# Retention and a gated MLP in one kernel: the first positions' values loaded by position in fp32 by another queue, with keys, queries and idle products rearranged to match

## The chip, the cores and the metric

The kernel runs on one core of one Trainium2 chip. A core has TensorE (PE; its weight loads are listed as PEld), VectorE (DVE), ScalarE (ACT), GpSimd (POOL) and SyncE (SP, which here only issues transfers). [...] The metric is the device time of one execution in microseconds (us), as the median of several runs.

## What is computed

```python
B, H, S, D = 8, 8, 576, 64               # q, k, v: fp32 [B, H, S, D]
scores = D ** -0.5 * q @ k.T             # for each batch and head
gamma[h] = 1 - 2 ** (-5 - h)
ret = scores * (gamma[h] ** (i - j) where i >= j, else 0)
x = (ret @ v) put together as [B * S, H * D]      # 4608 x 512
h = x @ w_in                             # w_in  512 x 2048
g = h * clip(h + 3, 0, 6) / 6
out = g @ w_out                          # w_out 2048 x 512
```

## The kernel before, in words

The 576 positions of a batch are split into the first 64 (the code calls them heads, `TL` is 64) and four chunks of 128. The first 64 positions of all eight batches make up block 0 of 512 tokens; the eight blocks after it are one batch each. A block goes through attention, then through the up-products `ph` (PE, 16 units of 128 columns of `w_in`, each four pairs of 128x512 matmuls; ACT and DVE make `u` and `g` from each), then through the down-products `pd` or `pm` with `w_out`. For the blocks after block 0, attention inside a chunk is done directly, and what lies before the chunk comes from a running state. The state left by the first 64 positions is made by `head_states` from block 0's keys and values.

Each engine takes its instructions in exactly the order in which the code issues them (a manual schedule); strings such as "k0 D4 k1 D4 ... h0" write the order out by hand, where `k` is `keys_heads`, `h` is `head_states`, `D` is a down-product step, `c` casts a loaded chunk, `t` turns it. An engine that waits holds up all that is behind it in its own list, and that holds for the issue of transfers too.

What comes ahead of the first up-product is the start of the kernel, and the change is almost wholly there:

- `load_half` (L403-416) loads the first 64 positions of head pair `i`, for two heads one after the other. A row of a transfer is four positions of one batch, 1 KB. Key pair 0 and the queries come as fp32 by SP and ACT and are cast by DVE (`cast_heads`). Keys of the pairs 1 to 3 and all values come by POOL, cast to fp16 on the way. `after` makes a transfer wait until another one has landed: most wait until key pair 0 has (`keys`).
- The partition of such a tile is batch and position group, so `turn_heads` (L428-440) uses matmuls with a permutation (`by_chunk`) to get the head dimension onto partitions, sorted into four chunks of two batches each; ACT or DVE copies the result out of PSUM.
- `by_key` (L441-449) permutes the other way with 16 small matmuls for each pair: values into `vh` (`values_heads`, by an ACT copy of 128x512), and later keys into `kn` (`keys_heads`, two ACT multiplies of 128x512, each with one of the two batches set to zero by `only`). The rows of a chunk are then in the order of position group, batch, position, and the masks (`distances`, `mask_of_heads`) are made for that order. `others` (L138-145) multiplies the keys by their decay on POOL ahead of that.
- `scores_heads` (PE `hpa`, DVE's multiply by the mask), `inner_heads` (PE `hpo`, which needs all four chunks of `vh`, and a copy into `xT`), then the first four up units in turn.
- `idle_products` are PE matmuls of an identity whose result nobody reads.
- `win_piece` and `wout_piece` issue the eight pieces of the MLP's weights by POOL. `fetch` loads the chunks of the later blocks by SP; the first one waits until the third piece of `w_out` to be issued has landed.

Of the kernel before, what the change touches and what calls it, by code (L numbers as in the profile page):

```python
# [14 lines left out]
I32 = mybir.dt.int32  # L15
# [6 lines left out]
def kernel(  # L22
# [45 lines left out]
    ii = const.tile([P, NJ + 1], I32)  # L68
    ij = const.tile([P, NJ + 6], I32)
    fj = const.tile([P, NJ + 6], FP32)  # L70
    key, odd = fj[:, NJ + 3:NJ + 4], fj[:, NJ + 5:NJ + 6]
    arg = const.tile([P, NJ + 3, 2 * H], FP32)
    dec = const.tile([P, NJ + 3, 2 * H], FP32)
# [11 lines left out]
    only = const.tile([P, 2], FP32)  # L85
# [4 lines left out]
    def indices():  # L90
        nc.vector.memset(half, 0.5)
        nc.gpsimd.iota(ii[:, 0:NJ], pattern=[[0, NJ]], base=0, channel_multiplier=1)
        nc.gpsimd.iota(ii[:, NJ:NJ + 1], pattern=[[1, 1]], base=0, channel_multiplier=1)
# [3 lines left out]
        p_ = ii[:, NJ:NJ + 1]  # L97
        nc.vector.tensor_scalar(ij[:, 0:NJ], ii[:, 0:NJ], P - B, 1, ALU.bitwise_and, ALU.logical_shift_right)
        nc.vector.tensor_copy(ij[:, NJ:NJ + 1], p_)
        for e in range(2):  # L100
            nc.vector.tensor_scalar(ij[:, NJ + 1 + e:NJ + 2 + e], p_, SUB - 1, 1, ALU.bitwise_and,
                                    ALU.logical_shift_left)
        nc.vector.tensor_scalar(ij[:, NJ + 3:NJ + 4], p_, RP - 1, 2, ALU.bitwise_and, ALU.logical_shift_left)
        nc.vector.tensor_scalar(ij[:, NJ + 4:NJ + 5], p_, 5, None, ALU.logical_shift_right)
        nc.vector.tensor_scalar(ij[:, NJ + 5:NJ + 6], p_, 4, 1, ALU.logical_shift_right, ALU.bitwise_and)
        nc.vector.tensor_copy(fj, ij)
        nc.vector.tensor_tensor(fj[:, 0:NJ], fj[:, 0:NJ], query[:, 0:TL:RP], ALU.add)
        nc.vector.tensor_scalar(fj[:, NJ:NJ + 2], fj[:, NJ:NJ + 2], 1.0, -float(P // 2), ALU.mult, ALU.add)
        nc.vector.tensor_scalar(fj[:, NJ + 2:NJ + 3], fj[:, NJ + 2:NJ + 3], 1.0, 1.0 - float(P // 2), ALU.mult, ALU.add)
        nc.vector.tensor_copy(by_chunk.rearrange("p (c e r) -> p c e r", c=NCB, e=2),  # L110
                              ident16.rearrange("p (r e c) -> p c e r", e=2, c=NCB))

    def distances():
        nc.vector.memset(scale, float(np.log(D ** -0.5)))
        nc.vector.tensor_tensor(key, key, fj[:, NJ + 4:NJ + 5], ALU.add)
        nc.vector.scalar_tensor_tensor(out=key, in0=odd, scalar=float(TL), in1=key, op0=ALU.mult, op1=ALU.add)
# [11 lines left out]
    def decays():  # L128
        for h in range(H):
            lg = float(np.log(gamma[h]))  # L130
            nc.gpsimd.tensor_scalar(arg[:, :, h], fj[:, 0:NJ + 3], lg, float(np.log(D ** -0.5)),
                                    ALU.mult, ALU.add)
            nc.gpsimd.tensor_scalar(arg[:, :, H + h], fj[:, 0:NJ + 3], -lg, 0.0, ALU.mult, ALU.add)
        nc.scalar.activation(dec, arg, ACTF.Exp)
        nc.gpsimd.tensor_copy(only[:, 1:2], odd)
        nc.gpsimd.tensor_scalar(only[:, 0:1], odd, -1.0, 1.0, ALU.mult, ALU.add)

    def others():  # L138
        for i in range(NP):
            k16 = hd[i]["k"].rearrange("p e j d -> p j e d")  # L140
            dd = dec[:, 0:NJ, H + 2 * i:H + 2 * i + 2].unsqueeze(3).to_broadcast([P, NJ, 2, D])
            nc.gpsimd.tensor_tensor(k16, k16, dd, ALU.mult)
# [54 lines left out]
    def casts(c):  # L197
        dd = dec.unsqueeze(3).to_broadcast([P, NJ + 3, 2 * H, D])
# [5 lines left out]
        if c % 2 == 0:  # L204
            q16 = work.tile([P, 2, NP, 2, D], FP16, tag="q16", bufs=2, name=f"q16_{c}")
            for e in range(2):
                nc.gpsimd.tensor_tensor(by_head(q16[:, e]), in_rows(st[c]["fq"][:, :, e, :]),  # L207
                                        in_rows(dd[:, NJ + 1 + e, 0:H, :]), ALU.mult)
            st[c]["q16"] = q16
        nc.gpsimd.tensor_tensor(v16, st[c]["fv"], dd[:, NJ, H:2 * H, :], ALU.mult)  # L210
# [75 lines left out]
    def head_states(c):  # L286
        pu = psum.tile([P, 2, NP, D], FP32, tag="pp", name=f"pu{c}")
        for e in range(2):
            for i in range(NP):
# [4 lines left out]
        nc.scalar.copy(zh[c + NCB], pu[:, 1])  # L294
        nc.vector.tensor_tensor(zh[c], pu[:, 0], decay, ALU.mult)
        nc.gpsimd.tensor_tensor(zh[c + NCB], zh[c + NCB], decay, ALU.mult)
# [98 lines left out]
    kn = [ws[n].rearrange("p j n -> p (j n)").rearrange("p (i c x) -> p i c x", i=NP, c=NCB) for n in (1, 2)]  # L395
# [32 lines left out]
    def turn_heads(i, nm, copy):  # L428
# [5 lines left out]
        x, y = (NCB, 2 * RP) if nm == "k" else (2 * NCB, RP)  # L434
        t = half_tile(work, "qT", i, FP16, "hqT", bufs=3) if nm == "q" else work.tile(
            [P, H * D], FP16, tag="kT", bufs=4, name=f"hkT{i}")
        t = t.rearrange("p (x j y) -> p x j y", x=x, j=NJ)
        copy(t, pt.rearrange("p j (x y) -> p x j y", y=y))  # L438
        hd[i][nm + "T"] = t

    def by_key(i, nm):  # L441

        pv = psum.tile([P, NCB, 2, D], FP32, tag="pp", name=f"hp{nm}{i}")
        for c in range(NCB):
            for j in range(NJ):
                o = slice(2 * RP * j, 2 * RP * j + 2 * RP)
                nc.tensor.matmul(pv[o, c], by_chunk[:, 2 * RP * c:2 * RP * c + 2 * RP], hd[i][nm][:, :, j],  # L447
                                 start=True, stop=True)
        return pv

    def values_heads(i):
        nc.scalar.copy(vh[:, :, i], by_key(i, "v"))

    def keys_heads(i):
        pk = by_key(i, "k").rearrange("p c e d -> p c (e d)")
        for e in range(2):
            nc.scalar.mul(kn[e][:, i], pk, only[:, e:e + 1])

    def scores_heads(i):
# [3 lines left out]
        for c in range(NCB):  # L463
            for h2 in range(2):
                r = slice(h2 * D, h2 * D + D)
                nc.tensor.matmul(pa[h2][:, c, :], kT[r, c].rearrange("d j x -> d (j x)"),
                                 qT[r, 2 * c:2 * c + 2].rearrange("d e j r -> d (e j r)"), start=True, stop=True)
# [186 lines left out]
    def win_piece(n, parts=1):  # L654
        a, b = pieces_in[n]
        for i in range(parts):
            cc = slice(NP // parts * i, NP // parts * (i + 1))
            nc.gpsimd.dma_start(win16[n][:, cc], win_v[:, cc, BLK * a:BLK * b])
# [62 lines left out]
    with tc.manual_schedule(engines={ENG.PE, ENG.DVE, ENG.Pool, ENG.Activation, ENG.SP}):  # L721
# [47 lines left out]
        win_piece(1)  # L769
        values_heads(3)  # L770
# [15 lines left out]
        others()  # L786
# [78 lines left out]
```

## Time and profile before

| What | Value |
|---|---|
| median of 3 runs | 301.76 us (301.63 to 302.48) |
| the profiled execution, its own time | 302.47 us |
| its span in the profile | 300.7 us |
| PE busy | 288.2 us, 96% |
| DVE, ACT, POOL busy | 213.2, 196.2, 135.5 us |
| mean granted clock of PE | 0.989 of full speed |
| first up-product | 18.51 us |
| granted clock 0.5 | 14.19 to 21.01 us |
| first `fetch` | 33.50 us |

How to read the profile: times are from the start of the span. A line of the order in time gives the start, the length, the engine, the source line, the operation, the tile written and the tiles read, partitions x elements and type, and how many; in brackets stands how long the engine was idle before and what ended that. Engines overlap, and matmuls overlap each other, so groups of PE start before the one ahead of them is listed as ended. The granted clock is the share of full speed that PE was allowed. Of a DMA queue the profile gives packets, megabytes written and the time of the packets as a share of 16 engines; an engine can have more than one packet under way, so shares go over 100%. q0 is POOL's queue, q1 SP's, q10 ACT's.

### The profile page before, as it was taken

To read this page: it belongs to the slowest core of one execution; us is meant where nothing else is said; L and a number is where in the kernel's file an instruction comes from. 1 tells how busy PE (TensorE), PEld (TensorE's weight loads), DVE (VectorE), ACT (ScalarE), POOL (GpSimd) and SP (SyncE) were. 2 spreads that over 40 slices of the span, in tenths; PEclk is the share of its full clock that TensorE was granted. 3 is DMA by queue.
4 is the path that set the end of the run, shared out by engine and by line. 5 is a ranking of instruction groups with operands and counts; after the bars stand their busy time and mean duration, and the time that the engine had idled before them with its cause. 6 is when DMAs were issued, how large, how long until landed. Compare 5 with 4: busy or idle time off the path is not lost.

```text
span 300.7 us, 12600 instructions
## 1 busy us (share of the span) xinstructions
PE 288.2 (96%) x5538; PEld 219.6 (73%) x5538; DVE 213.2 (71%) x387; ACT 196.2 (65%) x361; POOL 135.5 (45%) x176
## 2 busy tenths in 40 slices
PE   5799999899999999999979999999999999999995
PEld 2457666787556667877858878789788977778894
DVE  4728736769895688788875797678768776647554
ACT  4648875899866687586757577657765674565420
POOL 7975068517751912539621962375238003100510
PEclk9969999999999999999999999999999999999999
DMA  6999999996899989998999799789707100200114
GB/s 153 178 196 215 194 251 215 219 224 163 176 205 214 192 193 224 152 220 197 238 236 182 147 258 139 164 182 240 147 4 144 72 2 17 104 25 2 72 72 140
DMA packets 119542, 47.86 MB, mean 159 GB/s; under 512 B 92352, under 2 KB 114880, under 8 KB 119488
## 3 DMA queue, kind: packets, MB, share of 16 engines
q1 hardware_dynamic: 114336, 41.56, 66.7%
q0 software_dynamic: 4720, 5.11, 10.4%
q8 instruction: 43, 0.70, 1.0%
q10 hardware_dynamic: 432, 0.39, 0.4%
q14 instruction: 11, 0.09, 0.1%
HBM read 36.70 MB, written 9.44 MB: 153 GB/s over the span
## 4 chain that ended last, share of the span: by engine, by line
PE 91%; ACT 2%; DMA 2%; DVE 2%; issue 1%; SPq 0%; DVEq 0%; ACTq 0%
PE ph L168 42%; PE pm L168 29%; PE pd L168 9%; PE po L246 4%; PE pa L246 3%; DMA hq<-in_q_dram 2%; PE pu L246 1%; PE ptk L168 1%; PE hptq L432 1%; PE hpo L479 1%; ACT hqT L438 1%; PE hpv L447 1%; PE ptq L168 1%; DVE hq L425 0%; ACT u L510 0%
## 5 line engine op out<-in xcount | busy, mean ns | idle before, releaser
L168 PE MATMUL ph<-xT,win 128*64 128x512 f16 (+1 forms) x1248 | 146.3, 366 | 1.2 <-issue 0.5
L512 DVE SCALAR_TENSOR_TENSOR g<-u,ph 128x512 f16<-128x512 f32 (+1 forms) x156 | 98.6, 643 | 55.1 <-ACT u L510 54.8
L510 ACT ACTIVATE u<-ph,half 128x512 f32<-128x512 f32 (+1 forms) x156 | 100.3, 660 | 44.5 <-PE ph L168 42.5
L168 PEld LDWEIGHTS <-win 128*64 128x64 f16 x1248 | 85.2, 137 | 27.8 <-issue 3.1
L168 PEld LDWEIGHTS <-g 128*64 128x64 f16 x928 | 51.7, 110 | 14.8 <-issue 0.4
L168 PEld LDWEIGHTS <-s 128*64 128x64 f16 x896 | 50.3, 110 | 10.2 <-issue 2.4
L330 POOL TENSOR_TENSOR z<-z,gpow 128x256 f32<-128x256 f32 x24 | 15.8, 659 | 72.2 <-DVE z L329 53.6
L168 PE MATMUL pm<-ws,s 128*64 128x256 f16 x672 | 45.6, 273 | 0.0
L591 POOL TENSOR_TENSOR u<-u,p 128x512 f32<-128x512 f32 x7 | 8.9, 1271 | 62.1 <-ACT u L631 55.8
L382 ACT CAST xT<-po 128x256 f16<-128x256 f32 (+1 forms) x44 | 22.5, 583 | 21.8 <-PE po L246 21.8
L207 POOL TENSOR_TENSOR q<-fq,dec 128x512 f16<-128x512 f32 x32 | 36.7, 1169 | 0.0
L210 POOL TENSOR_TENSOR v<-fv,dec 128x512 f16<-128x512 f32 x32 | 35.1, 1100 | 0.9 <-PE ph L168 0.9
L168 PE MATMUL pd<-wout,g 128*64 128x512 f16 x256 | 34.8, 382 | 0.1
L168 PE MATMUL pm<-wout,g 128*64 128x256 f16 x448 | 31.9, 273 | 0.0
L281 DVE TENSOR_TENSOR a<-pa,mask 128x256 f16<-128x256 f32 (+1 forms) x44 | 21.9, 540 | 7.9 <-PE pa L246 4.7
L203 ACT CAST k<-fk 128x512 f16<-128x512 f32 x32 | 19.9, 622 | 0.0
L527 DVE TENSOR_TENSOR s<-g 128x1024 f16<-128x1024 f16 x28 | 19.2, 689 | 0.2
L336 ACT CAST z<-z 128x512 f16<-128x512 f32 x24 | 14.9, 620 | 5.4 <-DVE z L326 5.0
L168 PE MATMUL pm<-wout,s 128*64 128x256 f16 x224 | 16.5, 273 | 1.8 <-issue 1.7
L168 PE MATMUL pm<-ws,g 128*64 128x256 f16 x224 | 16.6, 274 | 0.0
L527 DVE TENSOR_TENSOR s<-g,s 128x1024 f16<-128x1024 f16 x14 | 12.9, 922 | 0.0
L246 PE MATMUL po<-qT,z 64*64 64x64 f16 x512 | 12.5, 198 | 0.4 <-ACT z L339 0.3
(111 smaller groups left out, 267.5 us busy)
## 6 DMA issues: line engine op xcount, KB each, us to landing
fk<-in_k_dram SPq DMA_DIRECT2D x32, 256.0 KB, 4.5
fq<-in_q_dram SPq DMA_DIRECT2D x16, 512.0 KB, 5.9
fv<-in_v_dram SPq DMA_DIRECT2D x32, 256.0 KB, 5.2
out_dram<-o SPq DMA_DIRECT2D x14, 512.0 KB, 3.1
wout<-in_moe_w_out_dram POOLq DMA_DIRECT2D x4, 512.0 KB, 16.7
out_dram<-o SPq DMA_DIRECT2D x7, 256.0 KB, 5.4
win<-in_moe_w_in_dram POOLq DMA_DIRECT2D x3, 512.0 KB, 10.3
hq<-in_q_dram SPq DMA_DIRECT2D x6, 128.0 KB, 4.9
```

The lines of the kernel that those rows point to most:

```text
L168: nc.tensor.matmul(out[r], lhs[:, r], rhs, skip_group_check=True, **flags)
L203: nc.scalar.copy(by_head(k16), in_rows(st[c]["fk"]))
L207: nc.gpsimd.tensor_tensor(by_head(q16[:, e]), in_rows(st[c]["fq"][:, :, e, :]), in_rows(dd[:, NJ + 1 + e, 0:H, :]), ALU.mult)
L210: nc.gpsimd.tensor_tensor(v16, st[c]["fv"], dd[:, NJ, H:2 * H, :], ALU.mult)
L246: return lambda: nc.tensor.matmul(*args, skip_group_check=True, **flags)
L281: nc.vector.tensor_tensor(a16[:, a, 0:n].rearrange("p x i q -> p (x i) q"), pa[a].rearrange("p x i q -> p (x i) q"), m, ALU.mult)
L330: nc.gpsimd.tensor_tensor(new, new, decay, ALU.mult)
L336: nc.scalar.copy(z16, zs[c])
L382: nc.scalar.copy(xt[:, s], po[s].rearrange("p x n (e r) -> p x n e r", e=2))
L510: nc.scalar.activation(uu[:, 0:n], ph[:, 0:n], ACTF.Relu, bias=half, scale=1.0 / 6.0)
L512: nc.vector.scalar_tensor_tensor(out=g[:, hf, ths, jr, :], in0=by_half(uu), scalar=1.0, in1=by_half(ph), op0=ALU.min, op1=ALU.mult)
L527: nc.vector.tensor_tensor(*pend.popleft())
```

## The change

- The values of the first 64 positions are no longer loaded by `load_half`. `load_values` issues four transfers from SP, each for two chunks and one of the two batches of a chunk: 64 partitions (the positions), with 16 pieces of 256 bytes in each, into one fp32 tile `vf`. They stand in SP's queue behind the queries. [...]
- `values_heads(c)` is now one cast of chunk `c` from `vf` into `vh`: ACT for chunks 0 and 1, POOL for 2 and 3. In POOL's list the two stand behind the issue of `win` pieces 0 (two halves) and 1, and ahead of `win` 2 and 3 and `wout`. The 64 permuting matmuls and four ACT copies of the values are gone.
- The first piece of `win` waits until the last query transfer has landed.
- Rows of a chunk are now batch, then position. `turn_heads` writes keys in that order, the masks are made for it with fewer DVE instructions.
- `keys_heads` turns `kT` back by the identity (8 matmuls with 64 columns for each pair, in place of 16 with 32), and two ACT multiplies of half the size put in the decay. `others` becomes `decays_of_chunk`, without the four POOL multiplies of keys.
- `head_states` uses the two halves of the rows for the two batches (16 matmuls of 64x64 for each chunk, two banks) in place of 16 matmuls over 128 rows with zeros.
- In the schedule, queries are cast earlier, all copies of turned queries are ACT's, two masks are made earlier, and there are 13 idle products in place of 9: 5, 4, 1, 1, and 2 ahead of `inner_heads(0)`.

```diff
     def head_states(c):
-        pu = psum.tile([P, 2, NP, D], FP32, tag="pp", name=f"pu{c}")
-        for e in range(2):
-            for i in range(NP):
-                for a in range(2):
-                    j, h2 = divmod(i + NP * a, 2)
-                    nc.tensor.matmul(pu[rows(a), e, i], kn[e][:, j, c, h2 * D:h2 * D + D], vh[:, c, j, h2, :],
-                                     start=True, stop=True, skip_group_check=True)
...
+        pu = [psum.tile([P, NP, D], FP32, tag="pp", name=f"pu{e}_{c}") for e in range(2)]
+        todo = ([], [])
+        for i in range(NP):
+            for a in range(2):
+                j, h2 = divmod(i + NP * a, 2)
+                for e in range(2):
+                    todo[e].append(mm(pu[e][rows(a), i], kn[rows(e), j, c, h2 * D:h2 * D + D],
+                                      vh[rows(e), c, j, h2, :], start=True, stop=True))
+        in_turn(todo)
...
+    vf = gp.tile([P, NCB, H * D], FP32, tag="g", bufs=4, name="hv")
+
+    def load_values(c, n):
+
+        for e in range(2):
+            b = c + NCB * e
+            nc.sync.dma_start(vf[rows(e), c:c + n].rearrange("p c (h d) -> p (c h) d", h=H),
+                              v[b:b + n, :, 0:TL, :].rearrange("b h s d -> s (b h) d"))
+
+    def values_heads(c, copy):
+        copy(vh[:, c].rearrange("p i e d -> p (i e d)"), vf[:, c])
+
+    def keys_heads(i):
+        pk = psum.tile([P, NCB, 2, D], FP32, tag="pp", name=f"hpk{i}")
         for c in range(NCB):
...
+            product(pk[:, c].rearrange("p a d -> p (a d)"), hd[i]["kT"][:, c, :], ident16, start=True, stop=True)
+        for a in range(2):
+            nc.scalar.mul(kn[:, i, :, a * D:a * D + D], pk[:, :, a, :], dec[:, 0, H + 2 * i + a:H + 2 * i + a + 1])
...
         for i in (2, 3):
             for e in range(2):
-                load_half(i, "q", e, sp, keys)
-        for i, nm in ((1, "k"), (2, "k"), (3, "k"), (0, "v"), (1, "v"), (2, "v"), (3, "v")):
+                queries = load_half(i, "q", e, sp, keys)
+        load_values(0, 2)
+        load_values(2, 2)
+        for i in (1, 2, 3):
             for e in range(2):
-                load_half(i, nm, e, pool, None if (i, nm) == (1, "k") else keys)
-        win_piece(0, 2)
+                load_half(i, "k", e, pool, None if i == 1 else keys)
+        win_piece(0, 2, queries)
+        win_piece(1)
         distances()
         idle_products(5)
         mask_of_heads(0)
         cast_heads(0, "k", on_dve)
         turn_heads(0, "k", on_act)
         mask_of_heads(1)
-        idle_products(3)
+        idle_products(4)
         cast_heads(0, "q", on_dve)
-        turn_heads(0, "q", on_dve)
+        mask_of_heads(2)
+        turn_heads(0, "q", on_act)
+        cast_heads(1, "q", on_dve)
         turn_heads(1, "k", on_act)
-        mask_of_heads(2)
+        turn_heads(1, "q", on_act)
+        cast_heads(2, "q", on_dve)
+        scores_heads(0)
+        mask_of_heads(3)
         idle_products(1)
-        cast_heads(1, "q", on_dve)
-        turn_heads(1, "q", on_act)
-        mask_of_heads(3)
-        scores_heads(0)
-        cast_heads(2, "q", on_dve)
         turn_heads(2, "k", on_act)
+        turn_heads(2, "q", on_act)
+        cast_heads(3, "q", on_dve)
         scores_heads(1)
-        turn_heads(2, "q", on_act)
+        idle_products(1)
         turn_heads(3, "k", on_act)
-        cast_heads(3, "q", on_dve)
+        turn_heads(3, "q", on_act)
         scores_heads(2)
-        turn_heads(3, "q", on_act)
-        values_heads(0)
         scores_heads(3)
-        values_heads(1)
+        for c in range(NCB):
+            values_heads(c, on_act if c < 2 else pool.tensor_copy)
+        idle_products(2)
         inner_heads(0, on_act)
-        values_heads(2)
         inner_heads(1, on_act)
-        win_piece(1)
-        values_heads(3)
         inner_heads(2, on_dve)
```

More of the change, by code (lines that the diff above doesn't have):

```diff
@@ L67 @@
     RP = TL // NJ
[L68 to L73, printed above, removed]
+    ii = const.tile([P, 1], I32)
+    ij = const.tile([P, 6], I32)
+    fj = const.tile([P, 6], FP32)
+    key, odd = fj[:, 4:5], fj[:, 5:6]
+    arg = const.tile([P, 4, 2 * H], FP32)
+    dec = const.tile([P, 4, 2 * H], FP32)
     ident16 = const.tile([P, P], FP16)
@@ L96, in indices @@
         make_identity(nc, ident16)
[L97 to L99 removed]
+        nc.vector.tensor_scalar(ij[:, 0:1], ii, SUB - 1, None, ALU.bitwise_and)
+        nc.vector.tensor_copy(ij[:, 1:2], ii)
         for e in range(2):
[L101 to L105, printed above, removed]
+            nc.vector.tensor_scalar(ij[:, 2 + e:3 + e], ii, SUB - 1, 1, ALU.bitwise_and, ALU.logical_shift_left)
+        nc.vector.tensor_copy(ij[:, 4:5], ii)
+        nc.vector.tensor_scalar(ij[:, 5:6], ii, 6, None, ALU.logical_shift_right)
         nc.vector.tensor_copy(fj, ij)
[L107 to L109 removed]
+        nc.vector.tensor_scalar(fj[:, 1:3], fj[:, 1:3], 1.0, -float(P // 2), ALU.mult, ALU.add)
+        nc.vector.tensor_scalar(fj[:, 3:4], fj[:, 3:4], 1.0, 1.0 - float(P // 2), ALU.mult, ALU.add)
         nc.vector.tensor_copy(by_chunk.rearrange("p (c e r) -> p c e r", c=NCB, e=2),
@@ L286, in head_states @@
     def head_states(c):
-        pu = psum.tile([P, 2, NP, D], FP32, tag="pp", name=f"pu{c}")
-        for e in range(2):
-            for i in range(NP):
-                for a in range(2):
-                    j, h2 = divmod(i + NP * a, 2)
-                    nc.tensor.matmul(pu[rows(a), e, i], kn[e][:, j, c, h2 * D:h2 * D + D], vh[:, c, j, h2, :],
-                                     start=True, stop=True, skip_group_check=True)
-        nc.scalar.copy(zh[c + NCB], pu[:, 1])
-        nc.vector.tensor_tensor(zh[c], pu[:, 0], decay, ALU.mult)
+        pu = [psum.tile([P, NP, D], FP32, tag="pp", name=f"pu{e}_{c}") for e in range(2)]
[7 more added lines that the diff above has]
+        in_turn(todo)
+        nc.scalar.copy(zh[c + NCB], pu[1])
+        nc.vector.tensor_tensor(zh[c], pu[0], decay, ALU.mult)
         nc.gpsimd.tensor_tensor(zh[c + NCB], zh[c + NCB], decay, ALU.mult)
@@ L394 @@
     hd = {}
-    kn = [ws[n].rearrange("p j n -> p (j n)").rearrange("p (i c x) -> p i c x", i=NP, c=NCB) for n in (1, 2)]
+    kn = ws[1].rearrange("p j n -> p (j n)").rearrange("p (i c x) -> p i c x", i=NP, c=NCB)
     vh = ws[4].rearrange("p j n -> p (j n)").rearrange("p (c i e d) -> p c i e d", c=NCB, i=NP, e=2)
@@ L433, in turn_heads @@
                                  skip_group_check=True)
-        x, y = (NCB, 2 * RP) if nm == "k" else (2 * NCB, RP)
         t = half_tile(work, "qT", i, FP16, "hqT", bufs=3) if nm == "q" else work.tile(
             [P, H * D], FP16, tag="kT", bufs=4, name=f"hkT{i}")
[L437 to L443, printed above, removed]
-        for c in range(NCB):
[L445 to L457, printed above, removed]
+        if nm == "q":
+            copy(t.rearrange("p (x j r) -> p x j r", j=NJ, r=RP), pt.rearrange("p j (x r) -> p x j r", r=RP))
+        else:
+            copy(t.rearrange("p (x r j) -> p x r j", j=NJ, r=RP), pt.rearrange("p j (x r) -> p x r j", r=RP))
+        hd[i][nm + "T"] = t.rearrange("p (c y) -> p c y", c=NCB)
+    vf = gp.tile([P, NCB, H * D], FP32, tag="g", bufs=4, name="hv")
[8 more added lines that the diff above has]
+        pk = psum.tile([P, NCB, 2, D], FP32, tag="pp", name=f"hpk{i}")
+        for c in range(NCB):
+            product(pk[:, c].rearrange("p a d -> p (a d)"), hd[i]["kT"][:, c, :], ident16, start=True, stop=True)
+        for a in range(2):
+            nc.scalar.mul(kn[:, i, :, a * D:a * D + D], pk[:, :, a, :], dec[:, 0, H + 2 * i + a:H + 2 * i + a + 1])
     def scores_heads(i):
@@ L465, in scores_heads @@
                 r = slice(h2 * D, h2 * D + D)
-                nc.tensor.matmul(pa[h2][:, c, :], kT[r, c].rearrange("d j x -> d (j x)"),
-                                 qT[r, 2 * c:2 * c + 2].rearrange("d e j r -> d (e j r)"), start=True, stop=True)
+                nc.tensor.matmul(pa[h2][:, c, :], kT[r, c, :], qT[r, c, :], start=True, stop=True)
         for h2 in range(2):
@@ L651, in weight_sums, with win_piece @@
                 pend.append((ws[n][:, j, :], x[:, j, :], y[:, j, :], ALU.subtract))
-    def win_piece(n, parts=1):
+    def win_piece(n, parts=1, behind=None):
         a, b = pieces_in[n]
@@ L657, in win_piece @@
             cc = slice(NP // parts * i, NP // parts * (i + 1))
-            nc.gpsimd.dma_start(win16[n][:, cc], win_v[:, cc, BLK * a:BLK * b])
+            d = nc.gpsimd.dma_start(win16[n][:, cc], win_v[:, cc, BLK * a:BLK * b])
+            if behind is not None:
+                after(d, behind)
     def wout_piece(pc):
```

26 lines of the change are left out of this document (8 added, 18 removed).

## The prediction

> **What bounds the kernel now.** I read the page's busy times and slices first, then the chain of waits, then the first 40 us in order of time, and last the DMA queues and the granted clock in short stretches. On the page, TensorE (PE) is the bound of nearly the whole run, but not of its start:
>
> ```profile
> PE 288.2 (96%) x5538; PEld 219.6 (73%) x5538; DVE 213.2 (71%) x387; ACT 196.2 (65%) x361; POOL 135.5 (45%) x176
> ...
> PE   5799999899999999999979999999999999999995
> ...
> PEclk9969999999999999999999999999999999999999
> DMA  6999999996899989998999799789707100200114
> ```
>
> The third slice (15 to 22.5 us) has a clock of 0.6, and the DMA engines are loaded to the 27th slice. After 21.7 us PE has work at every moment up to 45 us, so a change of the start counts by the moment at which PE begins its stream of up-products (`ph`), corrected for the clock it has there. In order of time, PE around that moment:
>
> ```profile
> 14.76 0.61 PE L466 MATMUL hpa<-hqT,hkT 64*128 64x128 f16 x8 [0.24 <-ACT hqT L438]
> 15.30 0.62 PE L447 MATMUL hpv<-hv,by_chunk 128*32 128x128 f16 x16
> 15.85 0.64 PE L479 MATMUL hpo<-ha,ws 128*64 128x128 f16 x8
> ...
> 18.08 0.64 PE L479 MATMUL hpo<-ha,ws 128*64 128x128 f16 x8
> 18.51 3.13 PE L168 MATMUL ph<-xT,win 128*64 128x512 f16 x16
> ...
> 21.70 12.29 PE L168 MATMUL ph<-xT,win 128*64 128x512 f16 x112
> ```
>
> Sixteen matmuls (8 pairs) from 18.51 last until 21.48, 0.37 us a pair; the next 112 take 12.29, 0.219 a pair. The granted clock in short stretches says why: it fell at 14.19 and rose at 21.01.
>
> ```profile
> 14.20:14.50 0.30, 0.30 (x16) 0.11 (x5) 0.30 (x2) 0.30 (x1) 0.30 (x1) 0.50 1.35 137
> 14.50:14.80 0.30, 0.06 (x5) 0.08 (x4) 0.30 (x1) 0.30 (x2) 0.30 (x2) 0.50 0.86 113
> 14.80:17.60 2.80, 2.80 (x60) 1.87 (x63) 1.50 (x3) 2.03 (x4) 2.24 (x6) 0.50 1.11 173
> 17.60:21.00 3.40, 3.40 (x38) 1.78 (x38) 0.69 (x1) 1.19 (x3) 2.97 (x17) 0.50 1.24 205
> ```
>
> (After the stretch and its length: busy time and instructions of PE, PEld, DVE, ACT, POOL; clock; DMA share; GB/s.) It changed at 10.77, 14.19 and 21.01, steps of 3.41 and twice 3.41, and rose after a step without a gap (17.60 to 21.01), not after one with 0.24 us idle and short matmuls (14.19 to 17.60). Eight pairs at the full rate take 1.76 of the 2.97 us, so the slow clock costs 1.2: before begins its stream as if at 18.5 + 1.2 = **19.7** at full clock. I compare that number.
>
> **The change, part by part.**
>
> Values leave PE. The four `hpv` groups go. In the chain three of them hold 0.55 us each (1.65) between 15.3 and 18.1; one from 14.01 lies beside an ACT copy.
>
> Queries sooner. Chained by the rows: query cast 0 at 6.80 (its landing is unchanged), turned from 7.28, ACT copy 0.59 to 8.55, key copy 1 to 9.14, query 1 turned meanwhile, its copy to 9.87, masks 0.69, then four copies of 0.59 with the turns between: the last scores end at about 14.2, not 15.4. The four more idle products (13 for 9; 0.22 or 0.43 us each by the clock) stand in gaps of PE that the ACT copies make, so I cost them at nothing; uncovered, they cost at most 4 x 0.43 = 1.7.
>
> The values' new way. All four chunks of `vh` must be there before `inner_heads(0)` can end. Chunks 2 and 3 come by SP's last two loads and then one POOL copy each, in POOL's queue behind three issues of `win`, with two more and the four of `wout` behind them. So the question is when SP's loads land. The queues:
>
> ```profile
> q0 software_dynamic: 246, 0.11, 85.2%
> q1 hardware_dynamic: 157, 0.14, 43.2%
> ...
> q0 software_dynamic: 395, 0.18, 141.2%
> ...
> q0 software_dynamic: 203, 0.20, 125.3%
> ...
> q1 hardware_dynamic: 867, 0.22, 137.2%
> ```
>
> These are packets, MB and share in 1 us: both queues at 9 to 10 us (POOL's keys and values, SP's queries); POOL's values alone at 11; `win` alone at 18; SP's 256-byte pieces of `fk` and `fv` alone at 39. A packet costs 55 ns of an engine for a head by POOL (0.852 x 16 us / 246), 44 for queries, 98 for `win`, 25 for a 256-byte piece. The new loads are 4 x 1024 pieces of 256 bytes, alone 4096 / 867 = 4.7 us; the old ones were 1024 packets, 1024 / 395 = 2.6.
>
> At 7.0 us, by the cumulated rows, 434 key packets (POOL) and 371 query packets (SP) are left: 40 us of engine time, at share 1.27 on 16 engines 2.0 us. So queries and keys are through at 9.0, and landed at 9.4 (last packet to landing took about 0.35; before: 10.55). The values flow from 9.0. POOL then issues two pieces of `win0` and `win1` (0.74 each, to 11.6); first packets 2.1 us after an issue, as POOL's first had (1.84 to 3.97), so at 11.5. By then 2.5 x 867 = 2170 pieces are through, chunks 0 and 1 among them, and 1930 are left, all of chunks 2 and 3, against 1024 packets of `win`. What they get is not in the trace of before, which has no 256-byte pieces beside `win`. Bounds: undisturbed, 1930 / 867 = 2.2 us more, landed at **14.0**; one packet for one packet, a pair costs 123 ns, 16 engines at 1.37 do 177 pairs a us, 1024 pairs last to 17.3 and the other 906 pieces to 18.3, landed at **18.7**; equal bytes, 110 GB/s for 0.49 MB, **16.1**. The nearest row (246 to 157, both queued) shows packets shared nearly one for one or better for POOL's. I take 17.5, towards that end.
>
> The trace's 256-byte row carries 217 GB/s against the 203 of `win` after halving its bytes, so per input byte it runs at about half. [...]
>
> POOL's copies of 128x512 from fp32 have no row. Above, the multiply 128x512 f32 (L207, 1.04); below, half of that, the 128x256 (L296, 0.61). I take 0.8. Chunk 3 is ready at 17.5 + 1.6 = 19.1. PE then ends inner 0 (0.15), does inner 1 and 2 (0.55 each, as above) and begins `ph` at **20.35**, 1.85 us later than before; `win0` has landed.
>
> The clock. With scores over at 14.2 and two idle products, PE stands from about 15 to 19. The step 17.60 to 21.01 then has 1.4 us idle, and the next rise is at 24.42: 4.07 us at half clock cost 2.0. The stream begins as if at 22.4, **+2.7**.
>
> Behind it. Four key turns become 8 matmuls of 128x128 with 64 columns; such a group (`ptk`) holds PE 0.22, the old `hpk` 0.34: -0.12 x 4. Head states go from 0.25 a group to half to nearly all of that (64*64 groups of the same count, 0.13 to 0.22): take -0.07 x 4. Together **-0.75**, all in the stretch 34 to 43 where PE has no gap. ACT's 8 multiplies of 128x512 (0.625) become 8 of half that size, POOL loses 4 x 1.04 at 25.8: both beside PE, no gain. POOL issues the last `win` and `wout` pieces only after its copies, from 19.1 instead of 13.3; the queue is empty from about 18 to 21, and `wout` and the loads of chunk 4 behind it come some 1 to 2 us later, about as much as PE. `decays` ends by some 28 us, and ACT needs it before its fifth `u`: PE's six banks hide that.
>
> **Sum**: +2.7 - 0.75 = +1.95. The profiled execution (302.47, span 300.7 and 1.8 around it) would become 304.4; it lies 0.7 above the median, so from 301.76 I say **303.7 us**.
>
> **Rivals.**
>
> Values undisturbed (faster). Landed at 14.0, copied by 15.6, `ph` from 16.85. If the clock still rises only at 21.0, the stream begins as if at 18.9: -0.8 - 0.75 = -1.5, 300.2. If the idle products close the gap so that it rises at 17.6, PE would gain 2.4 + 0.75, but then the loads hold: chunk 6's queries land at about 47.2 (issued 40.14, 7.1 us), POOL casts them from 48.47, so 1.3 us is free there, and about 0.6 more as PE's turn does not yet wait for that cast; some 299.8. For it: SP's loads are queued before `win` is even issued. Against: the shared row.
>
> In between (no change). Equal bytes: landed at 16.1, copied by 17.7, `ph` from 18.95, and as PE is then busy from 17.7 on, the clock rises at 21.0: as if at 20.0, +0.3 - 0.75 = -0.45, 301.3. [...]
>
> The change does not do what it says: queries that land no sooner leave the scores at 15.4; still beside the wait for values, so nothing in the main case, +0.6 in the faster one.
>
> **How the numbers follow.** About 0.3% (0.9 us) is what a measurement can tell from no change: faster is below 300.85, slower above 302.65. Forecast 0.47, undisturbed 0.34, between 0.19. Faster 0.34, same 0.19, slower 0.47. The forecast's own range: chunks landed at 17 with fast copies, about 302.7, to one-for-one sharing with copies of 1.04 (chunk 3 at 20.8, `ph` 22.05, clock up at 24.4: as if 23.2, +3.5 - 0.6), 304.7. The range must reach over the faster case: 299.5 to 304.9.
>
> **What would show it.** In the profile after: PE idle from about 15 until POOL's second copy; the landing of the last `hv` load near 17.5 and not 14; `ph` starting near 20 with LDWEIGHTS pairs 0.43 us apart until 24.4; key turns of 0.22. The forecast is wrong if POOL's copies begin before 15.5, or the clock is at 1.0 when `ph` begins.

## The result, and the profile after

Over 20 executions of each, the kernel before took 302.00 us in the median (300.84 to 303.21) and the changed one 303.67 (301.21 to 305.33): a ratio of 1.0063, 95% interval 1.0044 to 1.0082. The profiled execution of the changed kernel took 303.06 us, with a span of 301.3. The forecast was 303.7. The number was met, but partly by luck: the sum behind it lacked one term, which the experiments found.

The same lines of the page as before (instructions and busy time of each engine, then 40 slices of 7.5 us):

```profile
PE 287.0 (95%) x5450; PEld 220.7 (73%) x5450; DVE 211.8 (70%) x382; ACT 193.8 (64%) x360; POOL 128.0 (42%) x163
...
PE   6839999989999999999999999999999999999995
...
PEclk9978999999999999999999999999999999999999
DMA  6999999998999989998999999979928100210114
```

TensorE has 88 matmuls fewer. Its third slice, 15 to 22.5 us, fell from full to 0.3: it now stands there, while the DMA engines are loaded as before. In order of time, this is the changed kernel's start (start, length, engine, what; in brackets the idle time ahead and what ended it):

```profile
6.50 5.44 SPq L435 DMA_DIRECT2D hv<-in_v_dram  x4
...
11.26 2.22 POOL L646 DMA_DIRECT2D win<-in_moe_w_in_dram  x3 [4.92 <-DMA hq<-in_q_dram]
...
13.62 0.40 PE L455 MATMUL hpa<-hqT,hkT 64*128 64x128 f16 x8 [0.58 <-ACT hqT L424]
...
13.84 1.14 ACT L439 CAST ws<-hv 128x512 f16<-128x512 f32 x2 [0.26 <-DMA hv<-in_v_dram]
...
19.54 1.17 POOL L439 CAST ws<-hv 128x512 f16<-128x512 f32 x2 [6.06 <-DMA hv<-in_v_dram]
...
20.76 1.17 PE L467 MATMUL hpo<-ha,ws 128*64 128x128 f16 x18 [0.24 <-POOL ws L439]
...
21.75 3.61 PE L153 MATMUL ph<-xT,win 128*64 128x512 f16 x16
...
25.40 10.96 PE L153 MATMUL ph<-xT,win 128*64 128x512 f16 x99
```

The queries had landed by 11.26, where POOL's wait for `hq` ends. The scores ended at 14.02. POOL waited 6 us for the last values, which landed at about 19.4, its fourth issue of `win` behind them came at 20.65 (13.30 before), and the up-products began at 21.75, against 18.51 before. The clock (columns: stretch, length, busy time and count of PE, PEld, DVE, ACT, POOL, granted clock, DMA share, GB/s):

```profile
15.20:18.30 3.10, 0.07 (x2) 0.00 (x0) 0.48 (x1) 0.00 (x0) 0.00 (x0) 1.00 1.24 214
18.40:25.20 6.80, 4.76 (x38) 2.96 (x40) 0.69 (x1) 1.07 (x2) 5.40 (x12) 0.50 0.87 133
25.30:36.00 10.70, 10.70 (x109) 9.16 (x106) 7.82 (x13) 8.90 (x15) 3.10 (x24) 1.00 1.12 213
```

From 21.75 to 25.2 the stream ran at half clock. It began as if at 21.75 + 3.45 / 2 = 23.5 at full clock, against 18.51 + 2.50 / 2 = 19.8 before (the prediction, with a rougher rounding, has 19.7): 3.7 us lost. Aligned by ScalarE's instructions, the changed execution lies 3.7 us behind the one before from 23 to 31 us, and 3.24 from 47 to 130. Yet its span is only 0.6 longer. The 2.6 that come back are mostly this, in the execution **before** (PE around 154 us; "issue" is idle time that no wait explains):

```profile
152.30 1.95 PE L168 MATMUL ph<-xT,win 128*64 128x512 f16 x16
155.99 0.95 PE L168 MATMUL pm<-wout,s 128*64 128x256 f16 x14 [1.74 <-issue]
```

and in the **changed** one the same place:

```profile
155.76 1.95 PE L153 MATMUL ph<-xT,win 128*64 128x512 f16 x16
157.54 0.93 PE L153 MATMUL pm<-wout,s 128*64 128x256 f16 x14
```

A gap of 1.74 us is gone, and another of 0.53 at 199 us with it. The diff touches neither place. In the trace of before, a transfer of 16,384 bytes for instructions runs from 153.63 to 154.67, and PE stands from 154.25 to 155.99.

### The profile page after: what moved, and what is told of

Read it like the earlier page. It is cut to its first block, busy times and chain, and to the rows that moved or that the text cites. A ratio compares the mean times of both kernels' runs of the same rounds, so it can differ in the third digit from the quotient of the medians.

```text
span 301.3 us, 12401 instructions
## 1 busy us (share of the span) xinstructions
PE 287.0 (95%) x5450; PEld 220.7 (73%) x5450; DVE 211.8 (70%) x382; ACT 193.8 (64%) x360; POOL 128.0 (42%) x163
## 4 chain that ended last, share of the span: by engine, by line
PE 89%; DMA 5%; ACT 2%; SPq 1%; DVE 1%; issue 0%; POOL 0%; ACTq 0%; POOLq 0%
PE ph L153 42%; PE pm L153 29%; PE pd L153 9%; PE po L231 4%; DMA hv<-in_v_dram 3%; PE pa L231 3%; DMA hq<-in_q_dram 2%; PE pu L231 1%; SPq L435 1%; PE ptk L153 1%; PE ptq L153 1%; SPq L399 1%; PE hpo L467 0%; ACT u L498 0%; DVE qT L211 0%; DVE g L500 0%
## 5 line engine op out<-in xcount | busy, mean ns | idle before, releaser
L369 ACT CAST xT<-po 128x256 f16<-128x256 f32 (+1 forms) x44 | 22.5, 583 | 21.5 <-PE po L231 21.5
L153 PE MATMUL pm<-wout,g 128*64 128x256 f16 x448 | 31.1, 273 | 0.0
L266 DVE TENSOR_TENSOR a<-pa,mask 128x256 f16<-128x256 f32 (+1 forms) x44 | 21.9, 540 | 7.9 <-PE pa L231 4.2
L188 ACT CAST k<-fk 128x512 f16<-128x512 f32 x32 | 19.8, 620 | 0.0
L153 PE MATMUL pm<-ws,g 128*64 128x256 f16 x224 | 16.7, 274 | 0.0
```

What stands on the lines that cost most here:

```text
L153: nc.tensor.matmul(out[r], lhs[:, r], rhs, skip_group_check=True, **flags)
L188: nc.scalar.copy(by_head(k16), in_rows(st[c]["fk"]))
L266: nc.vector.tensor_tensor(a16[:, a, 0:n].rearrange("p x i q -> p (x i) q"), pa[a].rearrange("p x i q -> p (x i) q"), m, ALU.mult)
L369: nc.scalar.copy(xt[:, s], po[s].rearrange("p x n (e r) -> p x n e r", e=2))
```

## The experiments

For each kernel with a profile, the table gives the start of the stream of up-products (as if at full clock: half the time that it ran at half clock added), PE's gaps ahead of which nothing was waited for, the span, and the ratio to before on the same chip. A start includes waits for the first weights. e5 and e8 load other values than the output needs, so they give times only.

| kernel | start as if | gaps | span | ratio (95% interval) |
|---|---|---|---|---|
| before | 19.8 | 2.3 | 300.7 | 1 |
| changed | 23.5 | 0 | 301.3 | 1.0063 (1.0044 to 1.0082) |
| e1 weights behind values | 23.5 | 0.5 | 302.6 | 1.0138 (1.0091 to 1.0184) |
| e2 copies on VectorE | 22.2 | 0.3 | 300.3 | 1.0041 (1.0013 to 1.0069) |
| e3 25 idle products | 21.9 | 1.4 | 302.2 | 1.0031 (1.0003 to 1.0059) |
| e4 new order alone | 16.7 | 1.7 | 298.1 | 1.0058 (1.0029 to 1.0088) |
| e5 1024-byte pieces | 19.0 | 0.5 | 297.7 | 0.9964 (0.9940 to 0.9988) |
| e6 e2 and 19 idle products | 20.4 | 2.3 | 301.4 | 1.0060 (1.0033 to 1.0087) |
| e7 e4 again | 18.9 | 2.7 | 300.6 | single run |
| e8 loads of full height | 20.3 | 0.3 | 298.3 | single run |
| e9 e2 and 18 wide idle products | 19.5 | 1.4 | 299.2 | 1.0005 (0.9973 to 1.0036) |
| e10 before, 80 instructions more | 18.9 | 0.2 | 297.8 | 0.9960 (0.9935 to 0.9985) |
| e11 changed, 176 more | 21.0 | 1.6 | 301.0 | 1.0089 (1.0059 to 1.0118) |
| e12 e4, 72 more | 17.3 | 0.3 | 298.9 | 0.9951 (0.9925 to 0.9978) |

Span less start less gaps is 277.7 to 279.0 us in twelve of the fourteen rows; the two earliest starts, e4 and e12, have 279.7 and 281.3 (e12 has 1.5 us of another wait, shown below). So start and gaps carry nearly all of the difference in the other rows. A single profile is one draw, since clock and landings differ between executions, so the ratios, not the spans, say what a kernel costs.

**e1: the weights wait for the values.** In the changed kernel:

```diff
-        load_values(2, 2)
+        values = load_values(2, 2)
...
-        win_piece(0, 2, queries)
+        win_piece(0, 2, values)
```

> The changed kernel with one edit: the first piece of win waits for the last values load instead of the last query load. Theory (sharing): in the changed kernel the last values load landed at 19.4 us because the packets of win went between its pieces; at 13.5 us some 1100 of its 4096 pieces were left, which alone need 1100 / 760 = 1.5 us. So here it lands by about 15.3. POOL then issues win (0.74 x 3) ahead of its two casts of 0.6, so chunk 3 is ready at about 18.8 and the up-products begin at about 20.2 instead of 21.75; 302.2 to 302.7 us, ratio to before 1.00 to 1.003. Rival (the loads themselves): 256-byte pieces on 64 partitions, the last one issued only at 10.7, are that slow by themselves; then it lands at 18 or later, the up-products begin at 22 or later, and the time is 304 or more.

The last values landed at 17.0 (POOL's wait for them ends at 17.29), between the two forecasts, with no weight beside them. In the changed kernel's profile they landed 2.4 us later, so sharing is at most a part of the loss: even alone these loads took 3 us more than the 14.0 of the undisturbed case. The wait put POOL's copies behind three issues of weights (19.49) and all later loads 2 us later: 1.0138.

**e2: chunks 2 and 3 copied by VectorE.**

```diff
-            values_heads(c, on_act if c < 2 else pool.tensor_copy)
+            values_heads(c, on_act if c < 2 else on_dve)
```

> The changed kernel with one edit: chunks 2 and 3 of the values are cast by DVE instead of POOL. Theory (sharing): the loads still land at about 19.4, DVE's casts take 0.43 each instead of 0.6, so the up-products begin 0.3 us sooner, at about 21.4; POOL issues the rest of win and wout at about 13.5 instead of 20.7, so the first fetch comes some 4 us sooner than in the changed kernel, and that buys nothing, because no wait of PE for a load was seen there: 303.0 to 303.6 us. Rival (POOL's queue): holding back win and wout behind the casts is what costs; then this kernel returns to 302.0 or below.

VectorE's copy takes 0.43 against POOL's 0.61. The stream began at 20.05, at half clock until 24.44. The ratio fell by 0.0022, within the intervals of both. The first `fetch` came at 34.40, 2.5 us sooner than in the changed kernel (36.87), and the ratio did not come back to 1, so the weights held back behind POOL's copies are not the main cost.

**e3: 25 idle products ahead of the first inner products**, in place of 2.

> The changed kernel with one edit: 25 idle products instead of 2 ahead of the first inner product, so that PE stays busy from 14 until about 19.5 while it waits for the values. Theory (clock): the up-products still begin at about 21.7, but at full clock, 0.22 us a pair instead of 0.43; the 8 pairs ahead of the last inner product take 1.8 instead of 3.4 us, so 1.6 us is won: 301.9 to 302.4 us. Rival (the clock's rise does not hang on PE's being busy then): the pairs still take 0.43 us and the time is that of the changed kernel, 303.4 to 303.9. If the products run at half clock they take 10.7 us and end at 24.6, and the kernel is 2 to 3 us slower than the changed one.

The clock held: sixteen up-products from 21.94 took 1.95 us, against 3.61 in the changed kernel. This is not one execution's chance: the mean granted clock of the twelve executions lies between 0.993 and 1.000, and none of the changed kernel's twenty is above 0.989. The held clock is worth 1.6 us at the start; the ratio fell by 0.003, 1 us. The gaps of PE, none in the changed kernel, were 1.4.

**e4: the kernel before with the new order of queries, masks and idle products alone**, its values as before.

> The kernel before with one part of the change alone: queries cast and turned sooner, copies of turned queries by ACT, masks sooner, idle products 5, 4, 1 and 1 instead of 5, 3 and 1; values, keys and states stay as before. Theory: the scores end about 1.1 us sooner, as the changed kernel's did (14.0 instead of 15.4), the up-products begin at 17.4 to 17.8 instead of 18.5, and at half clock until 21.0 half of that is kept: 301.2 to 301.7 us, 0.3 to 0.8 below before. Rival: the chain of value matmuls and copies behind the scores, or the landing of the first half of win (about 16.6), sets the begin, and nothing is gained (301.8 to 302.2).

The profiled execution began its stream 3 us sooner than before and was the fastest of 12 (300.17); the median was 303.07, slower than before by 0.58%. A part of the change that shortens the start by itself lengthened the run. This is where the theory of the start alone fell.

**e5: values in 1024-byte pieces.**

```diff
-            nc.sync.dma_start(vf[rows(e), c:c + n].rearrange("p c (h d) -> p (c h) d", h=H),
-                              v[b:b + n, :, 0:TL, :].rearrange("b h s d -> s (b h) d"))
+            nc.sync.dma_start(vf[rows(e), c:c + n].rearrange("p c (x y) -> p (c x) y", x=2),
+                              v[b, 0:4, 0:4 * TL, :].rearrange("h (r j) d -> r h (j d)", j=4))
```

> The changed kernel, but each of the four loads of values reads 1024-byte pieces (four rows of positions of four heads on each of 64 partitions) instead of 256-byte pieces: the same bytes, the same number of loads, the same queue, partitions and issues, a quarter of the pieces. It loads other values than the reference's, so its output is another; the work behind the loads is the same. Theory A, the size of the pieces sets how long the loads of values take (some 750 pieces a us were seen whether or not the weights shared the engines): the last values land at 13 to 14.5 us instead of 19.4, POOL's copies are over by 15.5 to 16, the stream of up-products begins at 16.5 to 17.5, and the time falls by 3 to 4 us, to a ratio of 0.993 to 0.997 to before. Theory B, what holds them is their issue behind the queries and the sharing with the weights, by bytes: they land at 17 or later and the ratio stays at 1.004 to 1.008.

The queues from 12 to 13 us (packets, MB, share of an engine), in the changed kernel

```profile
q1 hardware_dynamic: 757, 0.19, 139.1%
```

and in e5

```profile
q1 hardware_dynamic: 247, 0.24, 111.7%
```

256-byte pieces hold an engine 1.391 x 16 / 757 = 29 ns each, 1024-byte pieces 72 ns, 2.5 times as long for four times the bytes. SP's issues of the values took (ns: shortest, median, longest; then first and last start in us), in the changed kernel and in e5:

```profile
L435 SPq DMA_DIRECT2D hv<-in_v_dram x4: 631/944/2788, 6.5 to 10.7; - x4
...
L435 SPq DMA_DIRECT2D hv<-in_v_dram x4: 596/608/631, 6.3 to 8.7; - x4
```

So the small pieces also held up the issue: the third one took 2.8 us, and the fourth began at 10.73, though the transfer that it waits for in the trace (the first of query pair 2) had landed at 8.17. In e5 it began at 8.66. Why the issue takes that long is not shown. The values of e5 landed at 15.7, later than theory A said but not at 19.4, and the ratio is 0.9964: the size of the pieces is worth 1% of the run, 3 us, about the whole loss at the start. In the microsecond shown, SP's queue moved 0.19 MB with the small pieces and 0.24 with the large ones.

**e6: e2 and 19 idle products together.**

> The changed kernel with both mendings together: chunks 2 and 3 of the values copied by VectorE, and 19 idle products instead of 2 ahead of the first inner products, so that TensorE has work from 14 until the values are there near 18.5. If copies and clock are what two thirds of the loss consist of, and are independent: the stream begins near 20 us at the full clock, as if at 20.0 against 23.6 in the changed kernel and 19.7 in the one before; the ratio to before is 0.998 to 1.002. Rival: the loss behind the start (later loads, or waits for instructions) is as large as that at the start, and the ratio stays at 1.003 to 1.006 as with either mending alone.

The stream began at 20.38 at full clock, 3.1 us sooner (as if) than in the changed kernel, and the ratio was 1.0060, the same as the changed kernel's. The profile has 2.3 us of gaps, with nothing to wait for:

```profile
171.22 0.63 PE L153 MATMUL pm<-ws,g 128*64 128x256 f16 x8 [1.43 <-issue]
...
184.10 0.34 PE L231 MATMUL po<-a,v 64*64 64x64 f16 x18 [0.61 <-issue]
```

**e7: e4 once more, for its profile.**

> The kernel before with the new order of queries, masks and idle products alone, a second time, for its profile: the first one was the fastest of its 12 executions (300.17 us, median 303.07), began its stream at 15.95 at full clock, and had 1.7 us of gaps of TensorE that no wait explains. Theory: a typical execution begins as early, and loses 3 to 4 us later, in such gaps or waits for loads, which this profile then shows. Rival: the start itself varies by this much (clock or landing of the weights), and the stream begins at 18 us or later.

Both held in part: the start came at 17.20 at half clock, and the gap near 154 us was the longest of all.

```profile
155.34 0.81 PE L168 MATMUL ph<-xT,win 128*64 128x512 f16 x5 [2.36 <-issue]
```

Counting PE's matmuls and weight loads from the start, the gap lies behind the 5816th in before and the 5815th in e4 and e7. In before that is between `ph` and `pm`; in e4 and e7, which have 8 more ahead of it, it is between two `ph`. So it belongs to a place in the stream, not to an operation. The instructions come in transfers of 16 KB, 43 in before to 11,076 matmuls and weight loads, 42 in the changed kernel to 10,900: 258 and 260 each by division. From these I take 256, an estimate, which the counts at the gaps (below) fit (the queue's rows on the two pages):

```profile
q8 instruction: 43, 0.70, 1.0%
...
q8 instruction: 42, 0.69, 1.0%
```

**e8: one load for each chunk, on all 128 partitions**, of the same 1024 pieces.

```diff
-        for e in range(2):
-            b = c + NCB * e
-            nc.sync.dma_start(vf[rows(e), c:c + n].rearrange("p c (h d) -> p (c h) d", h=H),
-                              v[b:b + n, :, 0:TL, :].rearrange("b h s d -> s (b h) d"))
+        for cc in range(c, c + n):
+            nc.sync.dma_start(vf[:, cc].rearrange("p (h d) -> p h d", h=H),
+                              v[cc, :, 0:2 * TL, :].rearrange("h s d -> s h d"))
```

> The changed kernel, but each of the four loads of values writes one chunk on all 128 partitions (positions 0 to 127 of eight heads) instead of two chunks on 64: the same 1024 pieces of 256 bytes a load. It loads other values than the reference's for the upper half, so its output is another. If transfers to half the partitions are slower in themselves, the pieces run at about 870 a us, as a chunk's keys do in the steady part, instead of 750, and the last values land by about 18 us instead of 19.4; if the height does not matter, they land at 19 to 19.8.

The values landed at 17.3, 2 us sooner than in the changed kernel, but e9 and e11, with the half-height loads, had them at 16.9. What orders these numbers is when POOL issued its weights: issued at 11.19 to 11.44 the values landed at 18.6 to 19.7 (e6, changed, e3), at 11.71 at 18.1 (e2), at 11.83 and later at 16.9 to 17.3 (e9, e8, e11, e1). So e8 shows nothing for the height. The row of landings fits the sharing, with weights 0.6 us sooner costing the values about 2, but it does not prove it: each is one execution, and the weights that e9 and e11 issued at 11.83 and 12.39 cost nothing against e1, which had none.

**e9: both mendings without the added instructions.** The idle products (3, 3, 1, 1 and 18) are single matmuls:

```diff
-            product(idle, ident16, ident16.unsqueeze(1).to_broadcast([P, NP, P]), start=True, stop=True)
+            nc.tensor.matmul(idle, ident16, ident16.unsqueeze(1).to_broadcast([P, NP, P]), start=True, stop=True)
```

> The changed kernel with both mendings (chunks 2 and 3 copied by VectorE, TensorE busy until the values are there), but its idle products, 3, 3, 1, 1 and 18, are single matmuls of 128 columns of weights instead of pairs of 64, so that TensorE's stream has as many instructions up to the values' products as the changed kernel's (52 in idle products) and not 68 more. Theory L (layout): the pair of mendings was worth 3 us at the start, and what took it back, 2.3 us of gaps of TensorE without a wait, comes from where the stream of instructions is cut into the 16 KB pieces in which it is loaded; with the changed kernel's count the gaps are gone: at most 0.6 us of them in the profile, and a ratio to before of 0.996 to 1.001. Rival S (the sooner start): a stream that starts sooner or never loses its clock meets the gaps whatever its count; they stay at 1.5 to 2.5 us, and the ratio at 1.004 to 1.007.

The ratio, 1.0005, is in theory L's range and 0.55% below e6's (the two intervals just touch). The gaps were 1.4 us, more than the 0.6 that L allowed, but in three pieces of at most 0.54. Part of the 0.55% is also a start 0.9 us sooner, since the values landed earlier here.

**e10: the kernel before, 80 instructions of PE more.** Its idle products are cut into narrower ones of the same columns in all (each is two matmuls and two weight loads):

```diff
-        idle_products(5)
+        idle_products(*[P] * 20)
...
-        idle_products(3)
+        idle_products(4 * P, P, P, P, P, 2 * P, P, P)
```

> The kernel before, with 80 more instructions of TensorE ahead of everything that counts: its first idle products are cut into four narrower ones each, with the same columns and nearly the same time. [...] Theory L: the gap of 1.7 to 2.4 us behind the 5814th instruction near 154 us, in all three profiles of kernels with the old values path, is gone or below 0.6, and the time falls by 1.5 to 2.5 us: ratio 0.991 to 0.996. Rival S: the gap belongs to the code there, not to the count; it stays, and the ratio is 0.998 to 1.002.

The gap near 154 us is gone:

```profile
151.67 1.95 PE L168 MATMUL ph<-xT,win 128*64 128x512 f16 x16
153.45 0.93 PE L168 MATMUL pm<-wout,s 128*64 128x256 f16 x14
```

The ratio is 0.9960, at the edge of theory L's range: cutting idle products made the kernel 1.2 us faster than it was. 80 is 256 (the estimate above) less 176, the matmuls and weight loads that the change removes (88 of each), so by that estimate this kernel's stream is cut where the changed one's is.

**e11: the changed kernel, 176 instructions more**, its 13 idle products cut into 57 of the same columns in all.

> The changed kernel, with 176 more instructions of TensorE ahead of everything that counts (its 13 idle products cut into 57 narrower ones, with nearly the same columns in all), so that the pieces of the stream are cut at the same code as in the kernel before. Theory L: a gap of 1.5 to 2.5 us appears near 157 us, and the time rises by as much: ratio to before 1.010 to 1.015. Rival S, and the rival that the changed kernel lacks the gap for another reason (its fewer loads or its later start): no gap above 0.6, ratio 1.004 to 1.008.

The gap appeared where theory L put it, behind the 5818th instruction:

```profile
155.28 0.27 PE L153 MATMUL pm<-wout,s 128*64 128x256 f16 x1
156.97 0.95 PE L153 MATMUL pm<-wout,s 128*64 128x256 f16 x13 [1.42 <-issue]
```

The ratio, 1.0089, lies between the two theories' ranges, and its interval overlaps the changed kernel's: the time alone would not settle it, the line does. The values landed at 16.9 in this execution, so its start was 2.5 us sooner than in the profile of the changed kernel; whether that is so in the median too is open.

**e12: the new order alone, with the stream cut as in e10.**

> The kernel before with the new order of queries, masks and idle products alone (as in e4), and its first idle products cut into narrower ones, so that TensorE has 72 instructions more than there up to its first up-product: 80 more than the kernel before, where e10 showed no gap near 154 us. By theory L the gap of 1.5 to 2.4 us is gone here too, so e4's ratio of 1.0058 falls by 0.005 to 0.008, to 0.998 to 1.001 at the most; what it then stands below or above e10 (0.996) is what the sooner queries alone are worth. If they are worth what the starts of the two profiles show (the stream began at 15.95 and 17.20, against 18.51 before and 17.52 in e10), 0.3 to 1.5 us, the ratio is 0.991 to 0.995. Rival: the stream then waits for its first weights instead (0.44 to 1.36 us in the two profiles, again in the second piece), the gain is nothing, and the ratio is 0.995 to 0.999.

The gap is gone (0.3 in all), and e4's 1.0058 became 0.9951 with nothing but narrower idle products: 1.1% of the run. Of the kernels that compute everything it is the lowest, 0.49% below before; from e10 it can't be told. The start, as if at 17.3, is 1.6 sooner than e10's, and this takes it back:

```profile
PE ptq L168 <- POOL q L207: 1.5, 2, 0.9
```

(In all, times, longest.) PE waits twice, 1.5 us together, for POOL's casts of fetched queries. The prediction gave that hold 1.3 to 1.9 us of slack in its faster case.

**The gaps of all fourteen profiles.** There are 23 gaps of PE of over 0.15 us that no wait explains. Each begins at a count of matmuls and weight loads that leaves between 178 and 191 when divided by 256, and each ends 1.2 to 1.6 us after the end of an instruction transfer. In before, the gap at 5816 (22 x 256 + 184) follows the 22nd of these transfers and the one at 7605 (29 x 256 + 181) the 29th. So, by these profiles, PE stands in these gaps for its next piece of instructions, and a gap ends once that piece is there: in before the 22nd transfer ended at 154.67 and the gap at 155.99.

## Why the prediction was right in its number and wrong in its sum

*Queries sooner.* Right: scores ended at 14.02 for 14.2.

*Queries and keys landed at 9.4.* Wrong. The packets ran on past 9.0: the last of the keys ended at 10.0 (POOL's 148 from 9 to 10 us are still keys) and the last of the queries at 10.35. They landed 0.6 us after it, where the reckoning had 0.35, and POOL went on at 11.26.

*Values at 867 pieces a us, landed at 17.5.* The mechanism was right, two sizes were off. The rate was some 750 (11 to 13 us), and the landing came 1.3 us behind the last packet, at 19.4. Alone they landed at 17.0 (e1), not at 14.0, so the rival of undisturbed values could not have won by keeping the weights away. Over the executions with these loads the landing lay between 16.9 and 19.7. How pieces share was put near one for one. From 14 to 15 us, and then from 15 to 16, the queues carried

```profile
q0 software_dynamic: 92, 0.09, 66.2%
q1 hardware_dynamic: 104, 0.03, 23.6%
...
q0 software_dynamic: 111, 0.10, 65.1%
q1 hardware_dynamic: 323, 0.08, 44.7%
```

In the first microsecond one piece went for one packet of weights, as the forecast assumed, and in the second three, nearly equal bytes, as the "in between" rival assumed. So neither assumption held throughout. The rival's time, 16.1, was also too early because it took the rate alone as 867.

*POOL's copies 0.8.* They took 0.61, the lower bound. `ph` began at 21.75, where the sum had 20.35.

*Clock, +2.7.* The rise was at 25.21 for 24.42, and the start's loss +3.7. The reason was right: PE was busy for 0.07 of the 3.10 us from 15.2 to 18.3, and from 18.4 on the clock was at 0.5; in e3, with PE kept busy, it held. The phase was not to be known: by the length of eight matmuls in the first products, 0.61 to 0.64 us at half clock and 0.40 or 0.41 at full, PE was at full clock by 7.19 us in e11 and still at half at 13.28 in e9.

*Behind it, -0.75.* The key turns gave more than their 0.48: from the first to the head states 4.92 us for 5.62. The head states, put at -0.28, cost 0.37, since the products after a group came later (spacing 1.02 for 0.90). Together -0.33 (ScalarE's instructions went from 3.71 us behind to 3.24). The first `fetch` was issued at 36.87 for 33.50, later than said, and without a wait.

*Not in the sum: instructions.* By the two profiles +3.7 - 0.33 - 2.27 = +1.1, where the spans differ by 0.6. That the forecast's +1.95 came near the medians' +1.67 is luck: the start was priced 1.0 too low, the steps behind it 0.4 too favourably, and the 2.3 us that the shorter stream gave back were not seen. They stood in the trace of before, as gaps that nothing explained at a place that the diff did not touch. Over the executions this place is worth less than in that one profile, 1.2 us (e10). With the stream cut alike, the change costs about 1%: 1.0063 against e10's 0.9960, 3.1 us, and 1.0089 (e11) against before, 2.7 us. That is the loss at the start, less what the steps behind it gave.

Open: why the transfer of instructions comes so late at this place and not at the others, why cutting the stream elsewhere is worth 3.2 us from e4 to e12 and only 1.2 from before to e10, why an issue of 256-byte pieces holds SP, and why e9's executions fall into eight near 300.5 and four near 303.3. Three of those four have a mean granted clock of 0.993 or 0.994, where the eight have 0.998 to 1.000: by an estimate from these shares, some 3.6 us more at half clock, which would cost 1.8 of the 2.8 us.

## What to carry to other kernels

When a load is put into another layout, count its contiguous pieces first: four times the pieces at a quarter of the size cost this kernel 3 us (changed against e5), more than the matmuls they replaced. With TensorE busy for 95% of the time, cutting the stream of instructions elsewhere was worth 1.1% from e4 to e12 and 0.4% from before to e10: look for idle time that nothing explains beside an instruction transfer. Before an edit that adds or removes many small instructions is judged, shift the stream with harmless ones (narrower idle products) and see whether the verdict stays.

## What was not expected of the hardware

A gap of 1.4 to 2.4 us of TensorE lay behind the 5815th to 5818th of its instructions in four profiles of three kernels (before, e4 and its repeat e7, e11), and was absent in the two that e10 and e12 made from them by 72 or 80 more. Of the 43 transfers of 16 KB in before, two left such a gap (1.74 and 0.53 us); the same kind of transfer left 2.36 us at one place in e7. Such gaps differ between executions of one kernel too (1.48 and 2.36 at the same place in e4 and e7).
